# Loading x transposed by DMA instead of transposing it on TensorE, in a fused attention and MLP kernel

## The chip, the cores and the metric

The kernel runs on one core of a Trainium2 chip. The metric is the device time of one execution in microseconds (us). The core has five engines that work side by side, each through its own list of instructions in order: TensorE (PE, matmuls; its weight loads are shown apart as PEld), VectorE (DVE), ScalarE (ACT), GpSimd (POOL) and SyncE (SP). Here SP does nothing but issue DMAs; ACT issues a few as well. The engines meet through semaphores, that the layer in which the kernel is written places.

## The reference

With x of 2048 rows and 640 columns in bf16, 32 heads of 20, and F = 1536:

```python
def _A_ref(x, wqkv, wo):
    qkv = (x @ wqkv).reshape(B, S, 3, H, Dh)      # transposed to 3, B, H, S, Dh
    q, k, v = qkv[0], qkv[1], qkv[2]
    p = softmax(einsum("bhqd,bhkd->bhqk", q, k) * Dh ** -0.5)
    return einsum("bhqk,bhkd->bhqd", p, v) @ wo    # heads put back side by side
def _B_ref(x, w1, b1, w2):
    h = x @ w1 + b1
    return (h * tanh(softplus(h))) @ w2
x = A_x
g = sigmoid((x * gate_w).sum(-1, keepdims=True))
return g * _A_ref(x, A_wqkv, A_wo) + (1 - g) * _B_ref(x, B_w1, B_b1, B_w2)
```

## The kernel before

The 2048 queries are taken in four chunks of 512 and the 32 heads in eight sets of four (one head in each 32 rows of the PE array), which makes 32 groups G, one for each set and chunk. A group has 16 key tiles of 128 keys, and for each tile four scores, one a head: 64 score units of 128 x 512. A unit takes one of two ways. In batches of two or three it is exponentiated on ScalarE (L1051, into `E`), and P times V takes `E` (L1068). Or VectorE turns the scores into the bits of a power of two (L556, into `T`), GpSimd adds shifts to those bits as whole numbers (L586), and PV takes the shifted copies with values scaled accordingly (`VD`, L538). The 16-bit sums land in a PSUM bank `acc`; with each value tile goes a column of ones, whose sum is the softmax's denominator.

Everything runs in an order written out in the string `ORDER` (L19), read token by token at L1268 and issued just so (`manual_schedule`): nothing moves at run time, and an engine that waits holds up all that comes behind on it. The tokens used below:

- `S n,k`: a batch of n scores on PE into banks from k on; `x`: its exp on ScalarE.
- `D G,j,r,k`: one score on PE for the way over VectorE, `d G,k,two` opens such a key tile, `p` is an addition on GpSimd, `y` the next piece of VectorE's work.
- `V j,i`: PV of a key tile, four matmuls.
- `C n,bank` takes up chain n of a list sorted by due time, and each `F` runs its next piece on PE (four matmuls beside each other, L633, or five transposes, L643). Chains are the projections (K and Q strips, V in `v_chain`), the MLP's two products and the output product; the last piece hands a copy to VectorE. `v_chain` of the first four heads multiplies x by `wv0`, whose 81st column is `gate_w`, so that the gate's sum comes with it.
- `q`, `k`, `o`, `b`: loads on SP of Q, K (which went through DRAM to change their layout), of the attention's output (`od`, loaded transposed, L890) and of the MLP's result. `e0` computes the gate, `e1` loads wo. `H` are filler matmuls.

All products with x need x transposed (`xT`, 5 blocks kt of 128 columns, for all 2048 rows). The kernel loads x as it is into `xs`, views of the tile `big` that the MLP uses later. Chunk 0 comes in four loads, alternating between SP and ACT (L444), and is transposed at the start (L1156 to L1167) on PE, 20 transposes of 128 x 128 through PSUM, two copies on VectorE and two on ScalarE. Chunks 1 to 3 are loaded on SP (L451) and transposed by chains of one piece each (`transpose_chain`, L637), with a copy on VectorE (L651).

Ahead of `ORDER` stand the first projections for the heads 0 to 3 and chunk 0 (L1182): K with all 512 keys, then Q, 128 columns wide, since the unused rows of K's weight tile `wkp` carry other columns of K (`w_top`), which `store_top` writes to DRAM. Then the scores begin. The loads at the start go, in order of issue on SP: x of chunk 0, K's weights, `w_top`, x of chunk 1, the gate column (L457), x of chunk 2, a strip of Q's weights, x of chunk 3, a strip of K's, all of V's, the MLP's bias, w1, further strips, w1 again, w2.

After the last group PE adds the last two head sets' output product to what was computed before (L1284); the last 128 x 4 rows are copied from PSUM by ScalarE (two whole rows of blocks and a half) and VectorE (three halves) and stored by SP.

Of the kernel before, what the change touches and what calls it, by code (L numbers as in the profile page):

```python
# [9 lines left out]
P = 128  # L10
# [3 lines left out]
BF16 = mybir.dt.bfloat16  # L14
# [5 lines left out]
S2,0 S2,2 C1,6 F x C2,5 F y1 x C3,4 F y2 S2,0 y3 C4,6 F x S3,2 y4 C5,5 F F F F x F F F F F F F F F F F F S2,0  # L20
F F S3,2 x F F C0,6 F F y5 x y6 F y7 F y8 y9 F S2,0 y10 V0,-1 x V1,-1 V2,-1 C6,6 F F F F F V3,-1 C7,5 F y11
C8,4 F y12 S2,0 S2,2 q1 C9,6 F y13 x C10,5 F y14 C11,4 F F x F F y15 F S2,0 F F F F x F F F S2,2 F F F F x F
S2,0 S2,5 F F F x y16 C12,3 F y17 y18 F y19 F y20 F x S3,0 F V4,-1 x V5,-1 y21 V6,-1 C13,6 F S3,3 y22 C14,2 F
x S2,0 y23 C15,6 F C16,2 F x y24 S3,3 y25 V7,-1 C17,6 F x F F F F F F F F F S2,0 F F F F x F S3,2 F F F F F
C18,5 F x F y26 y27 F y28 S2,0 y29 y30 F F x S2,2 y31 V8,-1 V9,-1 x V10,-1 d1,0,1 S2,0 S2,4 d1,1,0 D1,15,0,6
d1,2,0 d1,3,0 x C19,3 F y32 F F F x S3,0 D1,15,3,6 F y33 V11,-1 x S2,4 y34 C20,6 F F F F F F F F F F F x F
S3,0 D1,14,0,3 F F F y35 F F x F F F S2,4 y36 C21,3 F y37 y38 F y39 y40 e0 F v0 y41 F x S3,0 D1,15,1,6 q2 y42
V12,-1 y43 F V13,-1 x V14,-1 y44 S2,4 D1,14,3,6 C22,3 F y45 F F x F S2,0 D1,15,2,2 V15,-1 y46 F x F F S2,4
D1,13,0,6 y47 F p1,4 F F x C23,2 F F y48 F S2,0 F y51 F x S2,4 D1,13,3,6 y52 F y49 F y50 F F F x V0,-1 S2,0
D1,14,1,3 V1,-1 y53 x p2,-1 V15,0 S2,4 y55 C24,6 F y56 x F y57 F S2,0 D1,14,2,2 y54 d1,4,0 F x S2,3 D1,12,0,5  # L30
y58 F V2,-1 y59 x V15,1 p3,5 S2,0 D1,13,1,2 y60 V3,-1 V14,0 x y61 p4,0 S2,3 D1,12,3,5 C25,6 V14,1 y62 F x S2,0
D1,13,2,2 d2,1,0 F y63 F x S3,3 F p5,5 F x V4,-1 S2,0 D1,12,2,2 y64 V14,2 V13,0 y65 V5,-1 p6,0 x V13,1 S3,3
D1,12,1,6 d2,5,0 V6,-1 y66 C26,2 F x F F V13,2 F S2,0 D1,11,0,6 p7,2 F F y67 F x F q3 S2,3 D1,11,1,5 p8,0
V12,0 y68 F F x S2,0 D1,11,3,6 V7,-1 y69 V12,1 y70 x V12,2 y71 S2,2 D1,11,2,5 D2,15,1,4 d2,0,0 V8,-1 y72 x
C27,6 F F S2,0 F y73 p9,2 F F x F S2,2 D2,15,2,5 F F y74 F p10,3 F x S2,0 D2,15,0,4 V11,0 y75 V9,-1 y76 x
V11,1 y77 S2,2 D2,14,1,6 D2,14,2,5 V11,2 y78 x V10,-1 S2,0 D2,15,3,4 d2,2,0 y80 C28,6 F x F S2,2 y79 V0,-1 x
y81 F S2,0 D2,14,0,5 F y82 p11,3 y83 F x S2,2 D2,13,1,4 V1,-1 y85 V15,0 p12,4 x S2,0 D2,14,3,5 y86 d2,6,0
V15,1 C29,6 F y87 x F S2,2 D2,13,2,4 V15,2 y84 F F x y88 p13,1 F S2,0 D2,13,0,5 F F y89 F x F S2,2 D2,12,1,4
p14,3 F V2,-1 y90 V14,0 x S2,0 D2,13,3,5 y91 d3,4,0 C30,4 F F y92 F x F y93 F S2,2 D2,12,2,6 F F y94 F x F
S2,0 D2,12,0,5 V3,-1 y95 F x V14,1 S2,2 D2,11,1,6 y96 p15,1 V14,2 y97 V4,-1 x y98 S2,0 D2,12,3,5 d3,3,0 V13,0  # L40
y99 V5,-1 x S3,2 D2,11,2,6 p16,-1 V13,1 y100 V6,-1 x V12,0 p17,1 S2,0 D2,11,0,5 V13,2 y101 C32,6 F F p18,0 x F
S3,2 D2,11,3,5 d3,5,0 F y102 x F V7,-1 V12,1 y103 S2,0 D3,15,1,5 p19,1 V12,2 y104 V8,-1 x S3,2 D3,15,0,6 V11,0
p20,0 y105 V11,1 x S2,0 D3,15,2,5 V9,-1 y106 C31,6 F F F x S3,2 D3,14,1,5 V11,2 y107 F x F S2,0 y108 V10,-1
C33,5 F F y109 x F S3,2 D3,14,2,6 F y110 y111 x F V0,-1 S2,0 y113 C34,6 F F F y112 F F x F S3,2 D3,15,3,5 q4
d3,0,0 F F y114 F x F V1,-1 V2,-1 y115 S2,0 D3,13,1,5 p21,1 y116 V15,0 y117 C35,6 F x F S3,2 k1 p22,2 F F F F
x F S2,0 D3,14,3,5 F F y118 F V15,1 V3,-1 x V15,2 y119 S3,2 D3,12,1,5 y120 V4,-1 v1 y121 C36,6 F x F F y122
S2,0 D3,14,0,5 y123 F y124 F x S3,2 V5,-1 y125 p23,1 V14,0 x C37,5 F S2,0 D3,13,0,6 F p24,2 y126 F F x d4,4,0
F S3,2 D3,13,3,6 y127 V14,1 x V6,-1 V14,2 y128 S2,0 D3,13,2,5 q5 d4,1,0 V7,-1 y129 C43,6 F x F S2,2 D3,12,0,4
p25,2 F y130 F x S2,0 D3,12,2,5 F p26,3 y131 V13,0 x S3,2 V8,-1 y132 V13,1 x S2,0 D3,12,3,5 d4,2,1 V13,2 y133
V9,-1 C38,6 F F x F p27,3 S3,2 D4,15,1,5 F y134 x F V10,-1 p28,5 V12,0 y135 S2,0 D4,15,0,5 V12,1 y136 x V12,2  # L50
S3,2 D4,15,2,6 V11,-1 y137 x C39,5 F F F y138 S2,0 D4,14,0,6 F y140 x F S3,2 V0,-1 y141 C40,6 F x F F y139 F
S2,0 D4,14,1,5 y142 F V1,-1 y143 x S3,2 y144 C41,5 F F x S2,0 D4,15,3,6 d4,0,0 F y145 F F V2,-1 x S2,2
D4,13,0,6 D4,13,1,4 y146 p29,3 V3,-1 V15,0 y147 x S2,0 D4,14,2,5 p30,5 V15,1 y148 C42,6 F x F y149 S2,2
D4,12,0,4 F y150 x F S2,0 D4,14,3,5 d5,3,0 V4,-1 q6 y151 F x S3,2 V15,2 y152 p31,4 V5,-1 x S2,0 D4,13,3,5
V14,0 y153 C44,6 F p32,5 F F x S3,2 D4,13,2,5 F y154 F x S2,0 V14,1 y155 p33,1 V6,-1 V14,2 C45,5 F F x F S3,2
D4,12,3,6 y156 F F x V7,-1 V8,-1 S2,0 y157 H p34,-1 V13,0 y158 x S3,2 D5,15,0,6 C46,5 F y159 F x F F S2,0
D4,12,2,6 F y160 V13,1 x V9,-1 S2,2 D4,12,1,4 y161 d5,1,0 V10,-1 C48,6 F x y162 S2,0 D5,15,2,5 F y163 p35,2 F
x S2,2 D5,15,1,4 V11,-1 y164 F x p36,4 S2,0 D5,15,3,5 d5,5,0 F y165 d5,6,1 V12,0 x V12,1 S3,2 y166 p37,0 V12,2
x C47,5 F S2,0 D5,14,0,6 y167 F p38,2 F y168 F x F y169 S3,2 y170 V0,-1 V15,0 x S2,0 D5,14,1,6 y171 V15,1 q7
q8 y172 V1,-1 V15,2 C49,5 F x S3,2 D5,14,3,6 F y173 F x F F S2,0 D5,14,2,6 y174 d6,0,0 V2,-1 V3,-1 x S3,2 y175  # L60
D5,13,0,5 C50,6 F p39,2 x y176 F F F F S2,0 D5,13,2,5 y177 p40,3 V4,-1 x V14,0 y178 S3,2 D5,13,1,6 V14,1 y179
V5,-1 x S2,0 D5,13,3,5 d6,1,0 V14,2 y180 C51,6 F F F x S3,2 D5,12,2,5 p41,2 F y181 F x V6,-1 V13,0 p42,3 y182
S2,0 D5,12,0,5 V13,1 y183 C52,6 F x S2,2 D5,12,3,4 F y184 F x F S2,0 D5,12,1,5 d6,2,0 F y185 x V7,-1 S3,2
V13,2 y186 p43,4 V8,-1 x S2,0 D6,15,1,5 V9,-1 y188 C53,6 F F F x y187 S3,2 D6,15,0,5 q9 F F x S2,0 y189 V10,-1
p44,-1 V12,0 y190 C54,5 F F x F S2,2 D6,14,0,4 V11,-1 y191 F x F S2,0 D6,15,2,6 y192 V12,1 C55,4 F y193 x S2,2
# [1275 lines left out]
```

## Time and profile before

| what | us |
|---|---|
| median of 3 runs (lowest to highest) | 697.27 (696.99 to 698.68) |
| the profiled execution | 697.02 |
| its span in the profile | 695.2 |
| first score on PE / first exp on ScalarE | 10.04 / 10.47 |
| end of the last exp | 686.7 |
| busy: PE / ACT / DVE / POOL | 680.5 / 676.6 / 582.0 / 339.6 |

The profile is of one execution; its span leaves out 1.8 us that lie around it in the measured time. Rows give the line of the kernel, the engine, the operation, what it writes and reads, and how often; a row of the timeline begins with the start in us and the time it covers, merged over so many instructions. The shapes are partitions x elements. PE's matmuls overlap: a row's mean duration is longer than the distance between two starts, and the latter is what counts for throughput; ScalarE's instructions overlap a little as well. In a table of stretches, each engine's busy time is followed by its number of instructions, and the last three columns are the granted clock of PE, the share of time in which the DMA engines were busy, and GB/s. What an engine waited for is inferred from semaphores.

### The profile page before, as it was taken

The numbers are of one execution on the slowest core, as the hardware profiler recorded it, in microseconds if no ns is written. First come the engines' busy times: TensorE is split into PE (matmuls) and PEld (weight loads), VectorE is DVE, ScalarE is ACT, GpSimd is POOL, SyncE is SP. The second block draws the span as 40 slices with busy tenths as digits, with TensorE's granted clock in tenths as the row PEclk, the third lists the DMA queues.
The fourth block names the chain that finished last, engine by engine and source line by source line (L and its number), as shares of the span: only waits on it lengthen the run. The fifth ranks groups of instructions, "written<-read, shape, count | busy, mean of one in ns | idle before, by whom it ended". The sixth has DMA issues, their size and how long they took to land.

```text
span 695.2 us, 24441 instructions
## 1 busy us (share of the span) xinstructions
PE 680.5 (98%) x10325; PEld 240.0 (35%) x10325; DVE 582.0 (84%) x1009; ACT 676.6 (97%) x665; POOL 339.6 (49%) x334
## 2 busy tenths in 40 slices
PE   8999999999999999999999999999999999999997
PEld 4433333332323343333333222222234333343333
DVE  4488868888799888788898999988989988888896
ACT  5899999999999999999999999999999999999996
POOL 5025443435365434544547555554643565545543
PEclk9999999999999999999999999999999999999999
DMA  9612132313211212112031214232222121143221
GB/s 249 194 15 46 32 75 52 58 51 85 50 26 33 67 37 40 27 38 56 24 83 36 43 32 90 44 67 57 37 63 81 22 50 29 41 74 61 58 58 48
DMA packets 125613, 40.46 MB, mean 58 GB/s; under 512 B 91136, under 2 KB 124944, under 8 KB 125504
## 3 DMA queue, kind: packets, MB, share of 16 engines
q1 hardware_dynamic: 123904, 38.38, 24.7%
q8 instruction: 80, 1.31, 0.8%
q10 hardware_dynamic: 1600, 0.53, 0.3%
q14 instruction: 29, 0.24, 0.1%
HBM read 23.61 MB, written 12.79 MB: 52 GB/s over the span
## 4 chain that ended last, share of the span: by engine, by line
PE 78%; ACT 15%; DVE 3%; issue 3%; DMA 1%; SPq 0%; DVEq 0%; ACTq 0%
PE Sp L1033 26%; PE Sp L1068 26%; PE Sp L633 24%; ACT E L1051 11%; ACT big L840 3%; DVE T L556 2%; DMA w_top<-in_A_wqkv_dram 1%; PE Sp L1284 0%; ACT L1051 0%; PE Sp L1184 0%; DVE VD L538 0%; DVE big L819 0%; DVE T L1111 0%; PE Sp L643 0%; DVE bt L864 0%
## 5 line engine op out<-in xcount | busy, mean ns | idle before, releaser
L1051 ACT ACTIVATE E<-Sp 128x1024 bf16<-128x1024 f32 (+1 forms) x650 | 645.5, 1175 | 5.1 <-PE Sp L1033 4.0
L586 POOL INT64_ADD T<-T x320 | 330.4, 1043 | 340.6 <-DVE T L556 195.8
L556 DVE TENSOR_SCALAR T<-Sp 128x512 int16<-128x512 f32 x640 | 425.0, 685 | 76.9 <-PE Sp L1033 67.3
L1033 PE MATMUL Sp<-qT,kT 32*128 32x512 bf16 x2048 | 260.4, 383 | 6.2 <-ACT E L1051 3.0
L1033 PEld LDWEIGHTS <-kT 32*128 32x128 bf16 x2048 | 71.5, 91 | 240.5 <-issue 236.0
L1068 PE MATMUL Sp<-E,VA 128*21 128x512 bf16 x1408 | 133.9, 383 | 0.0
L1068 PE MATMUL Sp<-T,VD 128*21 128x512 bf16 x1252 | 117.4, 382 | 0.2
L633 PE MATMUL Sp<-w_sb,big 128*32 128x320 bf16 x1536 | 74.2, 301 | 0.6 <-DVE T L556 0.5
L633 PE MATMUL Sp<-xT,w1t 128*32 128x512 bf16 x960 | 73.4, 383 | 0.2
L1068 PEld LDWEIGHTS <-VA 128*21 128x21 bf16 x2048 | 45.5, 90 | 63.3 <-issue 54.2
L1068 PE MATMUL Sp<-T,VA 128*21 128x512 bf16 x640 | 62.4, 381 | 0.0
L633 PE MATMUL Sp<-xT,ws 128*32 128x512 bf16 x720 | 52.3, 381 | 0.2 <-ACT E L1051 0.2
L633 PEld LDWEIGHTS <-big 128*32 128x32 bf16 x1536 | 35.0, 95 | 28.0 <-issue 19.6
L1068 PEld LDWEIGHTS <-VD 128*21 128x21 bf16 x1252 | 30.8, 90 | 39.1 <-issue 32.7
L819 DVE TENSOR_SCALAR big<-Sp,b1f 128x512 bf16<-128x512 f32 x48 | 35.6, 741 | 1.5 <-PE Sp L633 1.1
L633 PE MATMUL Sp<-wv,xT 128*32 128x81 bf16 (+2 forms) x960 | 33.3, 257 | 0.4 <-DVE st L721 0.2
L633 PE MATMUL Sp<-wo_sb,od 128*32 128x320 bf16 (+1 forms) x608 | 28.9, 301 | 0.6 <-DVE T L556 0.6
L633 PEld LDWEIGHTS <-w1t 128*32 128x32 bf16 x960 | 20.1, 95 | 26.3 <-issue 19.4
L721 DVE CAST st<-Sp 128x512 bf16<-128x512 f32 x36 | 24.7, 685 | 5.3 <-PE Sp L633 5.2
L633 PEld LDWEIGHTS <-xT 128*32 128x32 bf16 x960 | 19.1, 96 | 12.8 <-issue 9.2
L777 DVE CAST VA<-Sp 128x80 bf16<-128x80 f32 (+2 forms) x48 | 16.2, 373 | 8.2 <-PE Sp L633 8.2
L633 PEld LDWEIGHTS <-ws 128*32 128x32 bf16 x720 | 16.8, 95 | 17.7 <-issue 10.0
(75 smaller groups left out, 206.1 us busy)
## 6 DMA issues: line engine op xcount, KB each, us to landing
w1t<-in_B_w_dram SPq DMA_DIRECT2D x24, 320.0 KB
q_dram<-st SPq DMA_DIRECT2D x20, 128.0 KB
b_dram<-bt SPq DMA_DIRECT2D x16, 160.0 KB
bl<-b_dram SPq DMA_DIRECT2D x16, 160.0 KB
out_dram<-ot SPq DMA_DIRECT2D x16, 160.0 KB
qT<-q_dram SPq DMA_DIRECT2D x124, 20.0 KB
o_dram<-T SPq DMA_DIRECT2D x120, 20.0 KB
kT<-k_dram SPq DMA_DIRECT2D x28, 80.0 KB
```

Of the source, the lines that this page charges most:

```text
L556: nc.vector.tensor_scalar(out=dst.bitcast(I16), in0=src, scalar1=inv_sqrt_dh * LOG2E * 128.0, scalar2=127.0 * 128.0 + (BETA2 if two else B ...
L586: nc.gpsimd.int64_add(dst[:, :].bitcast(I64), src[:, :].bitcast(I64), n * 0x0001000100010001)
L633: nc.tensor.matmul(out_[k : k + 32], lhsT=lhsT[:, k : k + 32], rhs=rhs, tile_position=(0, k), **kw)
L721: nc.vector.tensor_copy(out=res["st"][:, :], in_=ps[:, :])
L777: nc.vector.tensor_copy(out=VA[:, sts[i], h0 : h0 + nh, 0:DH], in_=ps[:, i, 0:n].rearrange("p (h d) -> p h d", d=DH),)
L819: nc.vector.tensor_scalar(out=big[:, pair_of(c, ft), (ft % 2) * QC : (ft % 2 + 1) * QC], in0=ps[:, :], scalar1=b1f[:, ft : ft + 1], scalar ...
L840: nc.scalar.activation(v, v, ACT.Mish)
L1033: nc.tensor.matmul(ps_cols, lhsT=kT[p][32 * t_ : 32 * t_ + 32, j * P : (j + 1) * P], rhs=qT[G][32 * t_ : 32 * t_ + 32, :], tile_position=( ...
L1051: nc.scalar.activation(E[:, x : x + n, :], allb[:, k0 : k0 + n, :], ACT.Exp, scale=inv_sqrt_dh,)
L1068: nc.tensor.matmul(acc[32 * t_ : 32 * t_ + DH + 1, :], lhsT=lhsT, rhs=rhs, start=(pv_done[G] == 0), stop=(pv_done[G] == pv_total[G] - 1), ...
```

## The change

x is loaded transposed by DMA: for every chunk and block one `dma_start(transpose=True)` of 512 rows x 128 columns (`load_x`). For chunk 0 the five blocks alternate between SP and ACT, and the first weights for Q and K are issued on ACT ahead of them; chunks 1 to 3 are issued on SP, with a strip of weights behind each of the first two, the gate column behind that of chunk 1, and V's weights at the end. The transposes on PE, their copies and the chains that held them are gone.

The first projections become K for 256 keys alone (`AHEAD`, with the unused rows of `wkp` zero) and Q, block by block as x arrives; `w_top` is put into `wkp` after that, and a chain `first_k_chain(0, ...)` computes K of all of chunk 0 a second time, with `w_top`, whose store moves there too. One filler matmul (`NFILL`) goes.

The bias, w1, w2 and the second strips are loaded in `load_rest`, called with the gate (`e0`). At the end each of four blocks of 128 rows gets one copy of 640 columns, two on ScalarE and two on VectorE, and the third is stored from ACT's queue.

`ORDER` is written anew. It holds 842 `V` (825 before), 668 `D` (640), 647 exps (650), of which 561 are of two units and 86 of three (542 and 108), 1216 `F` (1223), 334 additions on GpSimd (320) and no `H` (3). `FIRST` and `EARLY` could reorder the first group's key tiles and split `make_vd`; with the values given they change nothing.

```diff
-    for u in range(NU):
-        eng = nc.sync if u % 2 == 0 else nc.scalar
-        eng.dma_start(out=xs[0][:, u, :], in_=x2d[u * P : (u + 1) * P, :])
-    load_first(1, nc.sync)
+    def load_x(c, kt, eng):
+        eng.dma_start(
+            out=xT[:, kt, c * QC : (c + 1) * QC],
+            in_=x2d[c * QC : (c + 1) * QC, kt * P : (kt + 1) * P],
+            transpose=True,
+        )
+
     load_first(0, nc.scalar)
-    nc.sync.dma_start(out=w_top[:, :, :], in_=wrows[:, :, D + KTOP : 2 * D])
+    load_first(1, nc.scalar)
+    for kt in range(KT):
+        load_x(0, kt, nc.scalar if kt % 2 else nc.sync)
+    nc.scalar.dma_start(out=w_top[:, :, :], in_=wrows[:, :, D + KTOP : 2 * D])
     nc.scalar.dma_start(out=wv0[:, :, 0 : 4 * DH], in_=wrows[:, :, 2 * D : 2 * D + 4 * DH])
...
+    for c in range(1, NQC):
+        for kt in range(KT):
+            load_x(c, kt, nc.sync)
+        if c < NQC - 1:
+            load_strip(c - 1, 0, nc.sync)
+        if c == 1:
+            nc.sync.dma_start(
+                out=wv0[:, :, 4 * DH : 4 * DH + 1],
+                in_=gate_w.rearrange("(kt p o) -> p kt o", p=P, o=1),
+            )
     nc.sync.dma_start(out=wv[:, :, :], in_=wrows[:, :, 2 * D : 3 * D])
-    nc.sync.dma_start(b1bf, B_b1.rearrange("(ft p) -> p ft", p=P))
-    load_w1(0)
-    load_strip(0, 1, nc.sync)
-    load_strip(1, 1, nc.sync)
-    load_w1(1)
-    nc.sync.dma_start(out=w2_sb[:, :, :], in_=B_w2.rearrange("(ft p) c -> p ft c", p=P))
+
+    def load_rest():
+        load_strip(0, 1, nc.sync)
+        load_strip(1, 1, nc.sync)
+        nc.sync.dma_start(b1bf, B_b1.rearrange("(ft p) -> p ft", p=P))
+        load_w1(0)
+        load_w1(1)
+        nc.sync.dma_start(out=w2_sb[:, :, :], in_=B_w2.rearrange("(ft p) c -> p ft c", p=P))
...
-    sb = [bank_ap(g, [P, QC]) for g in (6, 2)]
+    pad_copy(wqp, w_first[0][:, :, :])
+    pad_copy(wkp, w_first[1][:, :, :])
...
-    for w, dst, k in ((wkp, kT[0][:, 0:QC], 0), (wqp, qT[0][:, :], 1)):
-        for kt in range(KT):
+    firsts = [
+        (bank_ap(4, [P, AHEAD]), wkp, kT[0][:, 0:AHEAD], nc.vector.tensor_copy),
+        (bank_ap(1, [P, QC]), wqp, qT[0][:, :], nc.scalar.copy),
+    ]
+    for kt in range(KT):
+        for ps, w, dst, _ in firsts:
             nc.tensor.matmul(
...
+    for ps, _, dst, copy in firsts:
+        copy(out=dst, in_=ps)
+    nc.vector.tensor_copy(
+        out=wkp[:, :, :, DH:32], in_=w_top[:, :, :].rearrange("p k (h d) -> p k h d", h=4)
+    )
...
     def gate_values():
+        load_rest()
...
+    finish(0, nc.scalar.copy, nc.sync)
+    finish(1, nc.vector.tensor_copy, nc.sync)
+    finish(2, nc.scalar.copy, nc.scalar)
+    finish(3, nc.vector.tensor_copy, nc.sync)
```

The new `ORDER` begins so, with the chains that stand behind the numbers C1 (K of chunk 0 again), C2 (`v_chain` of chunk 0, with the gate column), C0 (Q of chunk 1) and C3 (K of chunk 1):

```
S2,0 S2,2 C1,6 F x F F F F x C2,5 F F F F y1 F F F F F F F F S2,0 S2,2 F x F F F F F F F y3 S2,0 x y4 y5 y6 y7
y2 V0,-1 x S3,2 V1,-1 C0,6 F x F F F S2,0 F x C3,5 F F y8 F F F V2,-1 C4,6 F y9 F F F F F F F F F F F S3,0
```

More of the change, by code (lines that the diff above doesn't have):

```diff
@@ L25 @@
[L25 to L29, printed above, removed]
@@ L334 @@
     NSB = 2
-    NFILL = 1
+    FIRST = (0, 1, 2, 3, 4, 5, 6, 7, 8, 9, 10, 11, 12, 13, 14, 15)
+    EARLY = 16
+    AHEAD = 2 * P
     NSH = len(SHIFT) - 1
@@ L532, with tile_of, make_vd @@
     VD = {}
-    def make_vd(p):
-        VD[p] = work.tile([P, ND, NSH, 4 * (DH + 1)], BF16, tag=f"VD{p % NLAST}", name="VD")
+    def tile_of(p, j):
+        return FIRST[j] if p == 0 else j
+    def make_vd(p, part):
+        if p not in VD:
+            VD[p] = work.tile([P, ND, NSH, 4 * (DH + 1)], BF16, tag=f"VD{p % NLAST}", name="VD")
+        lo, hi = NS - ND, NS
+        if p == 0:
+            lo, hi = ((lo, EARLY), (EARLY, hi))[part]
+        j0 = tile_of(p, lo)
         def scale(i):
             nc.vector.tensor_scalar(
-                out=VD[p][:, :, i, :],
-                in0=VA[:, NS - ND : NS, 4 * p : 4 * p + 4, :].rearrange("p j h d -> p j (h d)"),
+                out=VD[p][:, lo - (NS - ND) : hi - (NS - ND), i, :],
+                in0=VA[:, j0 : j0 + hi - lo, 4 * p : 4 * p + 4, :].rearrange("p j h d -> p j (h d)"),
                 scalar1=RATIO[i + 1], scalar2=None, op0=ALU.mult,
@@ L953, in spread @@
         return [(a + (b - a) * k / n, a + (b - a) * (k + 1) / n) for k in range(n)]
+    chains.append(first_k_chain(0, -1.0, -0.3))
     for c in range(1, NQC):
-        for u in range(NU):
-            chains.append(transpose_chain(NU * c + u, -1.0, 0.25 * c - 0.2 + 0.01 * u))
         chains.append(first_k_chain(c, -1.0, 0.25 * c - 0.1))
@@ L1032, in score @@
         p = groups[G][0]
+        j = tile_of(p, j)
         nc.tensor.matmul(
@@ L1153 @@
     o_last = {}
[L1156 to L1179 removed]
+    pad_copy(wqp, w_first[0][:, :, :])
+    pad_copy(wkp, w_first[1][:, :, :])
     kT[0] = kTb[0]
     qT[0] = qTb[0]
[L1182 to L1183 removed]
+    firsts = [
[4 more added lines that the diff above has]
+        for ps, w, dst, _ in firsts:
             nc.tensor.matmul(
[L1185 removed]
+                ps,
                 lhsT=w[:, kt, :, :].rearrange("p h d -> p (h d)"),
[L1187 removed]
+                rhs=xT[:, kt, 0 : ps.shape[1]],
                 start=(kt == 0),
```

622 lines of the change are left out of this document (280 added, 342 removed).

## The prediction

> **What bounds the kernel now.** I read the page first, then the chain of waits, the groups by shape, the timelines of the start and of the end, and the transposing loads. The page's busy shares and its chain (the whole lines, three engines first):
>
> ```profile
> PE 680.5 (98%) x10325; PEld 240.0 (35%) x10325; DVE 582.0 (84%) x1009; ACT 676.6 (97%) x665; POOL 339.6 (49%) x334
> ...
> PE 78%; ACT 15%; DVE 3%; issue 3%; DMA 1%; SPq 0%; DVEq 0%; ACTq 0%
> ```
>
> TensorE (PE) is the bound, with ScalarE (ACT) close behind. A busy PE says little by itself, so I took the distances from one matmul's start to the next, slot by slot along ORDER. When nothing waits: one `V` (4 matmuls) 0.216 us, a piece `F` of 512 columns 0.216, of 320 0.136, of 240 0.103, of 81 0.039; a score batch `S` alone 0.32, but 0.007 when a `D` follows it (they run in the same pass), and that `D` 0.314; after an `F` or `V`, going to `S` costs 0.105 more. Added along the old list this gives 654.2 us; its first score starts at 10.04 and its last slot is 677.0 later. So 22.8 us are waits of PE, 9.9 of them in front of `S` or what then takes its bank.
>
> ScalarE, by shape; beside it the DVE work that takes its place:
>
> ```profile
> L1051 ACT ACTIVATE E<-Sp 128x1024 bf16<-128x1024 f32 x542 | 521.6, 1102 | 4.6 <-PE Sp L1033 3.7 <-ACT E L1051 0.2
> L556 DVE TENSOR_SCALAR T<-Sp 128x512 int16<-128x512 f32 x640 | 425.0, 685 | 76.9 <-PE Sp L1033 67.3 <-POOL T L586 1.3 <-issue 0.2
> ...
> L1051 ACT ACTIVATE E<-Sp 128x1536 bf16<-128x1536 f32 x108 | 166.6, 1543 | 0.5 <-PE Sp L1033 0.4
> ```
>
> Instructions overlap at their ends: back to back, an exp of 1024 starts 0.904 us after the one before, one of 1536 makes it 1.331. So the exps need 542 x 0.904 + 108 x 1.331 = 633.7 us.
>
> The start, from the timeline:
>
> ```profile
> 1.21 2.74 PE L493 MATMUL Sp<-qT 128*128 128x512 bf16 x6 [1.21 <-DVE qT L478]
> ...
> 4.26 0.51 SPq L457 DMA_DIRECT2D wv<-in_gate_w_dram  x1
> ...
> 7.03 1.25 PE L1184 MATMUL Sp<-xT,wkp 128*128 128x512 bf16 x5 [0.53 <-DVE wkp L1171]
> ...
> 8.12 1.24 PE L1184 MATMUL Sp<-xT,wqp 128*128 128x512 bf16 x5
> ...
> 10.04 0.40 PE L1033 MATMUL Sp<-qT,kT 32*128 32x512 bf16 x4 [0.67 <-ACT qT L1192]
> ...
> 10.47 7.38 ACT L1051 ACTIVATE E<-Sp 128x1024 bf16<-128x1024 f32 x7 [0.48 <-PE Sp L1033]
> ```
>
> The first exp is at 10.47, after x, its 20 transposes, K and Q. L493 spends 0.43 us per matmul, L1184 0.216 on the same width: PE starts at half pace, though the granted clock reads 1.00. The gate column is asked for at 4.26 and has landed by 9.6, before its first reader.
>
> Transposing loads, which the kernel has already for `od` (same block, 512 x 128 from rows of 1280 bytes). First answer: the timeline of SyncE (SP), two places; second: a table of stretches around the lone one:
>
> ```profile
> 489.05 5.12 SPq L890 DMA_TRANSPOSE od<-o_dram  x4
> ```
>
> ```profile
> 578.50 1.56 SPq L890 DMA_TRANSPOSE od<-o_dram  x1
> ```
>
> ```profile
> 579.50:580.00 0.50, 0.50 (x11) 0.22 (x11) 0.00 (x0) 0.50 (x1) 0.50 (x1) 1.00 0.35 82
> 580.00:580.50 0.50, 0.50 (x16) 0.21 (x8) 0.50 (x1) 0.50 (x2) 0.38 (x1) 1.00 0.79 173
> 580.50:581.00 0.50, 0.50 (x14) 0.23 (x14) 0.20 (x1) 0.50 (x1) 0.13 (x1) 1.00 0.06 7
> ```
>
> Issuing one holds its queue 1.2 to 1.3 us (a plain load: 0.4 to 0.5). The lone one moves its bytes between 579.5 and 580.7, and its completion counts are in by 581.2: 2.7 us from the start of its issue.
>
> **The change, part by part.**
>
> *The list.* The same distances along the new ORDER give 650.7, 3.5 less: the 12 transposes of later chunks go (-4.1); `V` 825 to 842, with their turns to `S` (+5.4); `D` 640 to 668 (+3.7); score batches, fewer of them alone (-6.3); five pieces more for K of chunk 0, the rest of that chunk's keys (+0.9); three `H` (-0.7); pieces of other widths, fewer turns (-2.3). ScalarE: 561 x 0.904 + 86 x 1.331 = 621.6, 12.1 less, since 28 more score units go over DVE. DVE gets 28 x 0.664 = 18.6 us more and loses 14 copies of 0.49; it idles 113 us, which covers it; were it not covered, it would cost these 12 us. POOL gets 14 adds of 1.04 and is half idle.
>
> What of ScalarE's 12.1 shows is bounded by nothing (PE leads the chain with 78%) and by all 9.9 of the waits in front of `S`. PE's work falls by 0.5%, ScalarE's by 1.9%, so I take half: -4.9.
>
> *x by DMA, chunk 0.* Five transposes, kt 0, 2, 4 on SP and 1, 3 on ACT. The trace of before has all its transposes on one queue, so it can't show what two queues do. Bounds: side by side, SP issues three in 3 x 1.25 us, so the last starts at 3.25 and lands at 5.95; one at a time, each issued when the one before it has landed, 0.73 + 5 x 2.7 = 14.2. I take the second: the code alternates the queues at every block, and I expect the layer that places this program's semaphores to put one in front of each change of queue; the trace of before doesn't decide it, hence the large chance of B below. [...]
>
> [...]
>
> From the last landing to the first score: before, the last Q matmul starts at 8.99 and the score at 10.04, 1.05; PE has been idle between blocks and may be at L493's pace, and a quarter of K comes too: 1.4. First score 15.6, against 10.04 (+5.6).
>
> *The gate column.* It moves behind the five transposes of chunk 1 and a weight strip on SP. SP starts kt 4 at 11.5; six transposes x 1.27 = 7.6; the strip 0.5: the gate load starts at 19.6 and lands, by the same 2.7, at 22.3. The new list puts v_chain of chunk 0 (C2), whose right-hand side holds that column, 1.4 us of work after the first score, at 17.0. PE runs in order, and behind C2's first piece stand the scores for the third and fourth exp. So all engines stop for 5.3 us; nothing covers it. [...]
>
> Chunk 1 has landed by 21 and its strip before the gate column; chunks 2 and 3 land near 29 and 35, wanted 9.8 and 15.5 us of work after 22.3. Covered by 3 us.
>
> *w1, w2, late strips with the gate (`e0`).* They leave the start of SP and come 28 us of work after the first score, in front of Q loads; a strip is wanted 24 us later, w1 55. 0; if the cover goes, the 6 us that 1.9 MB take at the 329 GB/s that the stretch from 20 to 25 us shows.
>
> *The end.*
>
> ```profile
> 690.12 1.29 ACT L1299 CAST ot<-Sp 128x640 bf16<-128x640 f32 x2 [3.42 <-PE Sp L1284]
> ...
> 690.68 1.29 DVE L1308 CAST ot<-Sp 128x320 bf16<-128x320 f32 x3 [0.47 <-PE Sp L1284]
> 690.84 0.93 SPq L1302 DMA_DIRECT2D out_dram<-ot  x2
> 691.29 0.44 ACT L1306 CAST ot<-Sp 128x320 bf16<-128x320 f32 x1
> 691.86 0.89 SPq L1310 DMA_DIRECT2D out_dram<-ot  x2
> ```
>
> SP issues the last store at 692.36. Two copies of 640 columns on each engine end near 691.9 (DVE: 0.82 each, from 0.69 for 512), and one store goes by ACT's queue: the last issue near 691.95, -0.4.
>
> **Sum**, against the profiled execution's 697.02 us (span 695.2 and 1.8 around it; the median of the runs is 697.27): 15.6 + 650.7 + 22.8 waits + 5.3 + 1.0 - 4.9 = 690.5 for the end of the list, before 687.0: +3.5; the end -0.4: +3.1. **700 us**.
>
> **The rivals.**
>
> *B, the transposes run side by side (other side).* First score 5.95 + 1.4 = 7.4; gate column issued at 4.5 + 6.35 + 0.5 = 11.35, landing 14.05, still a stop of 5.25. 7.4 + 673.5 + 5.25 + 1.0 - 4.9 = 682.3, -4.7, with the end -5.1: 692. For it: nothing in the trace of before shows such a wait. It decides when the second queue's transpose starts under 1.4 us after the first's. Without relief of ScalarE 697.
>
> *C, ScalarE paces the whole.* Most of its exps start exactly 0.904 apart, which speaks for it. Then all 12.1 us come back in place of 3.5 + 4.9: 3.7 better than the forecast, 696.3. Against: 78% PE.
>
> *D, SP jams.* After 20.1: ten transposes, 12.7, strip, wv, four o_dram stores (3.2), then 8 stores of K rows and the store and load of group 1's Q: landing between 47 and 53. Group 1's first score is 28.4 - 1.4 us of work after 22.3, 50.3 with the slow clock. At worst 3 to 4 us late, with both engines empty: 704. Before, these had no 20 slow issues ahead of them.
>
> **How the numbers follow.** Forecast 0.50, B 0.24, C 0.14, D 0.12. The forecast's own range is 697 to 704 (relief 0 to 9.9, slow clock 0 to 2). Range over all: 691 to 705.5. About 0.3%, 2.1 us, is what can be told from no change here. Slower by more: 0.37 of the forecast's 0.50, D's 0.12, 0.01 of C: 0.50. Faster: 0.20 of B, 0.04 of C, 0.02 of the forecast: 0.26. Within: 0.24.
>
> **What would show it.** Right: five transposes of x alternating on SP and ACT about 2.7 us apart, first exp near 16, an idle PE of some 5 us in front of the first xT x wv piece with the gate's load as its releaser, exps near 622 us at their own pace, a PE list near 651 plus waits. Wrong: transposes 1.25 us apart and the first exp near 8 (B); no stop at the gate column; or PE waits well off 18 to 23 us in the rest.

## The result, and the profile after

The changed kernel takes 707.27 us (median of 4 runs, 705.93 to 707.97), the kernel before 697.94 in the same session: 1.0135 times as long, with a 95% interval of 1.0123 to 1.0147. The prediction was 700.0 with a range of 691 to 705.5. The time lies above that range. So the sign was right and the size was not: +3.1 us was forecast, and in the profiled execution it is +10.4 (span 705.6 against 695.2).

The page, engines and the chain that ended last:

```profile
PE 676.8 (96%) x10320; PEld 236.1 (33%) x10320; DVE 588.7 (83%) x1021; ACT 665.1 (94%) x659; POOL 357.0 (51%) x349
...
PE 74%; ACT 14%; issue 3%; DVE 3%; DMA 3%; SPq 1%; DVEq 0%; ACTq 0%
```

Every engine that bounds the kernel is busy for less time than before (PE 680.5, ACT 676.6), and the span is longer: the time went into pauses. DMA and SP now hold 4% of the chain, 1% before. The exps, by shape:

```profile
L1043 ACT ACTIVATE E<-Sp 128x1024 bf16<-128x1024 f32 x561 | 535.3, 1088 | 15.5 <-PE Sp L1025 14.3
...
L1043 ACT ACTIVATE E<-Sp 128x1536 bf16<-128x1536 f32 x86 | 131.0, 1525 | 1.6 <-PE Sp L1025 1.6
```

In the kernel before, ScalarE idled 4.6 us ahead of its exps of 1024 (3.7 of them for PE); now it is 15.5 (14.3 for PE). Where, the chain of waits over the first 30 us shows (start, length, what held it):

```profile
0.73 1.23 SPq L445
...
3.30 3.09 DMA xT<-in_A_x_dram
...
6.50 2.67 DMA xT<-in_A_x_dram
...
9.19 2.52 DMA xT<-in_A_x_dram
...
11.73 2.67 DMA xT<-in_A_x_dram
...
14.47 1.12 SPq L445
...
20.18 3.03 DMA wv<-in_gate_w_dram
```

SP issues three blocks of x at its own pace (0.73, 2.01, 3.30). Then each change of queue waits until the transposes before it have landed: ACT at 6.50, SP at 9.19 (this is already a block of chunk 1), ACT at 11.73, SP at 14.47. The same start as a timeline, on PE and ScalarE:

```profile
16.55 0.61 PE L1025 MATMUL Sp<-qT,kT 32*128 32x512 bf16 x4 [0.67 <-ACT qT L1166]
17.09 2.32 PE L647 MATMUL Sp<-xT,wkp 128*32 128x512 bf16 x20
17.19 1.94 ACT L1043 ACTIVATE E<-Sp 128x1024 bf16<-128x1024 f32 x2 [0.70 <-PE Sp L1025]
...
23.25 1.01 PE L647 MATMUL Sp<-wv,xT 128*32 128x81 bf16 x48 [3.83 <-DMA wv<-in_gate_w_dram]
...
24.84 4.26 ACT L1043 ACTIVATE E<-Sp 128x1024 bf16<-128x1024 f32 x4 [5.71 <-PE Sp L1025]
```

First exp at 17.19 (10.47 before); the stop at the gate column is there, PE idle 3.8 us and ScalarE 5.7. The five `F` of C1 at 17.09 cover 2.32 us; at full pace they take 1.3 (0.216 each and the last one's length): PE is at half pace.

Laid out as the prediction's sum was, with distances between starts on PE and their minimum when nothing waits:

| part of the span, us | before | after | difference | predicted |
|---|---|---|---|---|
| first score starts | 10.04 | 16.55 | +6.5 | +5.6 |
| the list at its minimum | 654.2 | 650.65 | -3.5 | -3.5 |
| PE's waits up to 40 us | 2.9 | 7.9 | +5.0 | +6.3 |
| waits from 40 to 60 us | 0.9 | 4.2 | +3.3 | 0 |
| waits after 60 us | 19.0 | 17.1 | -1.9 | -4.9 |
| last slot to the end | 8.25 | 9.2 | +1.0 | -0.4 |
| sum | | | +10.4 | +3.1 |

The stop behind "from 40 to 60 us" is one the prediction didn't see. The timeline there:

```profile
54.16 0.26 ACT L1184 ACTIVATE g_t<-z_t 128x16 f32<-128x16 f32 x1
...
54.45 0.17 DVE L1185 TENSOR_SCALAR g_t<-g_t 128x16 f32<-128x16 f32 x1 [0.92 <-ACT g_t L1184]
...
55.03 0.69 DVE L713 CAST st<-Sp 128x512 bf16<-128x512 f32 x1
...
55.77 0.29 PE L647 MATMUL Sp<-wv,xT 128*32 128x240 bf16 x4 [1.81 <-DVE st L713]
```

The gate's steps stand in DVE's queue ahead of the copy that frees PE's bank, and their first one waits for the gate's exp, which stands in ScalarE's queue behind the exps of scores. And the stop is paid a second time, as a table of stretches shows (busy time and number of instructions of PE, PEld, DVE, ACT and POOL, then granted clock, DMA share, GB/s):

```profile
56.00:58.00 2.00, 2.00 (x38) 0.91 (x38) 1.19 (x3) 1.18 (x2) 0.00 (x0) 0.67 1.06 144
58.00:60.00 2.00, 2.00 (x27) 0.39 (x17) 1.79 (x4) 1.62 (x2) 1.39 (x2) 0.50 0.85 243
60.00:62.00 2.00, 2.00 (x54) 1.15 (x50) 1.81 (x4) 1.67 (x3) 0.67 (x1) 0.98 0.97 251
```

From 56.7 to 60.1 PE has half its clock, which makes 1.4 us more: of the 3.3 that this stretch lost, 1.9 are the stop and 1.4 the clock. e4 below has the same stop without the slow clock (its mean granted clock is 0.999) and loses 1.7 there against the kernel before.

The end, timeline:

```profile
698.00 1.11 PE L1259 MATMUL Sp<-wo,O 128*128 128x320 bf16 x7 [1.05 <-DVE big L928]
...
700.03 1.25 PE L1259 MATMUL Sp<-wo,O 128*128 128x320 bf16 x8
700.56 0.69 ACT L1276 CAST ot<-Sp 128x640 bf16<-128x640 f32 x1 [5.29 <-PE Sp L1259]
700.87 1.56 DVE L1276 CAST ot<-Sp 128x640 bf16<-128x640 f32 x2 [1.53 <-PE Sp L1259]
701.28 1.51 SPq L1279 DMA_DIRECT2D out_dram<-ot  x3
701.79 0.69 ACT L1276 CAST ot<-Sp 128x640 bf16<-128x640 f32 x1 [0.54 <-DVE ot L1276]
```

PE's final products wait 1.05 us for copies of the last output chains (C177 to C179), which the new list runs up to its last tokens. From the start of the last eight matmuls to the end of the span it is 5.56 us (5.66 before). ScalarE's second copy waits 0.54 for DVE's; no run shows why.

### The profile page after: what moved, and what is told of

The parts are those of the page before. It is cut to its first block, busy times and chain, and to the rows that moved or that the text cites. A ratio compares the mean times of both kernels' runs of the same rounds, so it can differ in the third digit from the quotient of the medians.

```text
span 705.6 us, 24501 instructions
## 1 busy us (share of the span) xinstructions
PE 676.8 (96%) x10320; PEld 236.1 (33%) x10320; DVE 588.7 (83%) x1021; ACT 665.1 (94%) x659; POOL 357.0 (51%) x349
## 4 chain that ended last, share of the span: by engine, by line
PE 74%; ACT 14%; issue 3%; DVE 3%; DMA 3%; SPq 1%; DVEq 0%; ACTq 0%
PE Sp L1060 25%; PE Sp L1025 25%; PE Sp L647 23%; ACT E L1043 13%; DVE T L570 2%; DMA xT<-in_A_x_dram 2%; ACT big L832 1%; SPq L445 1%; DMA q_dram<-st 1%; DMA wv<-in_gate_w_dram 0%; PE Sp L1259 0%; DVE st L713 0%; DVE big L811 0%; DVE T L1089 0%; DVE big L928 0%
## 5 line engine op out<-in xcount | busy, mean ns | idle before, releaser
L1043 ACT ACTIVATE E<-Sp 128x1024 bf16<-128x1024 f32 (+1 forms) x647 | 635.6, 1146 | 17.0 <-PE Sp L1025 15.9
L600 POOL INT64_ADD T<-T x334 | 347.2, 1051 | 324.8 <-DVE T L570 184.3
L570 DVE TENSOR_SCALAR T<-Sp 128x512 int16<-128x512 f32 x668 | 440.6, 684 | 63.2 <-PE Sp L1025 53.3
L1025 PE MATMUL Sp<-qT,kT 32*128 32x512 bf16 x2048 | 257.0, 386 | 5.9 <-DVE st L713 1.9
L1025 PEld LDWEIGHTS <-kT 32*128 32x128 bf16 x2048 | 68.9, 91 | 238.9 <-issue 235.9
L1060 PE MATMUL Sp<-T,VD 128*21 128x512 bf16 x1320 | 125.1, 382 | 0.0
L647 PE MATMUL Sp<-xT,w1t 128*32 128x512 bf16 x960 | 75.2, 383 | 0.1
L647 PE MATMUL Sp<-w_sb,big 128*32 128x320 bf16 x1536 | 72.5, 301 | 0.3 <-DVE ot L928 0.2
L1060 PE MATMUL Sp<-T,VA 128*21 128x512 bf16 x668 | 64.9, 382 | 0.0
L1060 PEld LDWEIGHTS <-VD 128*21 128x21 bf16 x1320 | 32.3, 90 | 39.1 <-issue 32.8
L647 PEld LDWEIGHTS <-ws 128*32 128x32 bf16 x720 | 17.0, 96 | 18.9 <-issue 10.2
```

Of the source, the lines that this page charges most:

```text
L570: nc.vector.tensor_scalar(out=dst.bitcast(I16), in0=src, scalar1=inv_sqrt_dh * LOG2E * 128.0, scalar2=127.0 * 128.0 + (BETA2 if two else B ...
L600: nc.gpsimd.int64_add(dst[:, :].bitcast(I64), src[:, :].bitcast(I64), n * 0x0001000100010001)
L647: nc.tensor.matmul(out_[k : k + 32], lhsT=lhsT[:, k : k + 32], rhs=rhs, tile_position=(0, k), **kw)
L1025: nc.tensor.matmul(ps_cols, lhsT=kT[p][32 * t_ : 32 * t_ + 32, j * P : (j + 1) * P], rhs=qT[G][32 * t_ : 32 * t_ + 32, :], tile_position=( ...
L1043: nc.scalar.activation(E[:, x : x + n, :], allb[:, k0 : k0 + n, :], ACT.Exp, scale=inv_sqrt_dh,)
L1060: nc.tensor.matmul(acc[32 * t_ : 32 * t_ + DH + 1, :], lhsT=lhsT, rhs=rhs, start=(pv_done[G] == 0), stop=(pv_done[G] == pv_total[G] - 1), ...
```

## Experiments

The ratios are against the kernel before, run beside each (medians 696.95 to 697.02). All but e11 start from the changed kernel, which was timed in a session where the kernel before took 1 us more; so differences from it are taken from ratios, or from e7, which lies within 0.04% of it by its ratio and ran beside e5, e6 and e8.

| kernel | us (lowest to highest) | ratio, 95% | first score | waits to 40 / 40 to 60 |
|---|---|---|---|---|
| e1_one_queue | 701.98 (701.06 to 703.18) | 1.0073 (1.0058 to 1.0088) | 10.12 | 9.6 / 3.2 |
| e2_gate_early | 700.95 (699.53 to 702.97) | 1.0059 (1.0036 to 1.0083) | 12.27 | 6.4 / 2.5 |
| e3_both | 701.27 (698.00 to 702.14) | 1.0069 (1.0052 to 1.0086) | 10.08 | 6.6 / 3.1 |
| e4_x_plain | 694.14 (692.18 to 695.64) | 0.9956 (0.9941 to 0.9972) | 10.50 | 3.2 / 2.6 |
| e5_filler | 706.38 (704.68 to 706.77) | 1.0129 (1.0112 to 1.0146) | 15.67 | 5.5 / 3.8 |
| e6_gate_steps_later | 704.71 (703.73 to 705.62) | 1.0109 (1.0094 to 1.0125) | 16.08 | 7.8 / 1.4 |
| e7_old_end | 706.62 (706.39 to 707.26) | 1.0139 (1.0123 to 1.0154) | 16.10 | 8.0 / 3.9 |
| e8_chunk0_on_PE | 695.25 (692.99 to 698.29) | 0.9973 (0.9955 to 0.9990) | 9.10 | 7.2 / 3.9 |
| e9_filler_more | 706.86 (704.05 to 707.33) | 1.0130 (1.0104 to 1.0156) | 15.71 | 2.1 / 5.5 |
| e10_best | 692.08 (691.56 to 692.93) | 0.9930 (0.9913 to 0.9948) | 8.92 | 4.5 / 0.8 |
| e11_exp_shorter | 690.36 (690.26 to 692.55) | 0.9913 (0.9896 to 0.9930) | 9.92 | 4.8 / 0.7 |
| e12_all_dma_mended | 695.37 (694.21 to 696.20) | 0.9974 (0.9963 to 0.9985) | 10.05 | 6.9 / 1.2 |

The last two columns are of the one profiled execution of each, and a wait counts where it begins (the stop of e8 at 40 us in the first of the two numbers). This execution isn't always a typical one: it is the fastest of e1, e2 and e3, and the slowest of e6, e8, e11 and e12.

**The queues and the gate column.** e1: `load_x(0, kt, nc.sync)` for all five blocks. e2: the gate column's `dma_start` moved ahead of the loop over chunks 1 to 3. e3: both.

> All five transposing loads of chunk 0 go on SP, nothing else changes. If the hand-over between the queues is what delays the start (each change of queue waits about 2.7 us for a landing), the five are issued 1.28 us apart, the last lands near 8.6, the first score comes near 10.0 instead of 16.55, and the gate column near 16.8 instead of 23.2, with the same stop of 4 to 5 us in front of it: about 700.8 us, 6.5 less than the changed kernel, still above the kernel before. If the DMA engines or HBM set the pace of the transposes, whatever the queue, the last block still lands near 14.4 and the time stays at 707.

> The gate column is loaded on SP ahead of the transposes of chunk 1, the blocks of chunk 0 still alternate. If the stop of PE from 18.8 to 23.2 is owed to the gate column, it goes, and the scores of the third exp follow the second at once: 4 us earlier there, and some of the half-paced matmuls after the pause with it. If nothing behind it is late, about 703; if the loads and stores queued on SP are late anyway (the staging tiles are freed by stores that stand behind the transposes), a later wait takes the gain back and the time stays near 707.

> One queue for chunk 0 and the gate column early. First score near 10, no stop at the gate: PE is some 10.5 us ahead of the changed kernel at its 20th exp. SP gains only the 6 us of the hand-overs, so the wait for a staging tile near the 40th exp (2.2 us in the changed kernel) should grow to some 5 or 6: about 700, little better than with one queue alone. If SP's queue is not what that wait is owed to, the gains add up: about 696.

e1 takes 4.3 us off (0.62 points of the ratio) and the first score comes 6.4 us earlier. But the gate column still stands behind chunk 1's five transposes and a strip, so the stop there grows from 4.3 to 5.8 us above its minimum:

```profile
17.34 1.01 PE L647 MATMUL Sp<-wv,xT 128*32 128x81 bf16 x48 [5.63 <-DMA wv<-in_gate_w_dram]
```

e2 does two things at once. The stop at the gate is gone, and ACT's two blocks go out together behind SP's three (issues at 6.10 and 7.33), since SP's next transpose now follows them: first score 12.27. e3 doesn't add the two gains. What follows is next in line: PE now stops 3.1 us at 14.8 for the first strip of Q's weights, which SP issues behind chunk 1's transposes, and 1.6 at 44.0 for group 1's Q, which stands further back on SP.

**No transposing at all.** e4: one plain load a chunk, gate early.

```diff
+            out=xT[:, :, c * QC : (c + 1) * QC],
+            in_=x2d[c * QC : (c + 1) * QC, :].rearrange("(p a) d -> p (a d)", p=P).rearrange("p (k q) -> p k q", q=QC),
```

> x is loaded by one plain load a chunk, into the shape of xT but not transposed, so all products with x have other values (the computation is the same in size); the gate column comes early. This takes the transposes' price away and leaves the new list and the new end. If the loads at the start are the whole loss: first score near 7, no wait for the gate, no wait for staging tiles, 650.7 us of list with some 19 of waits and 9 of end: about 688 us, 10 below the kernel before. If the new list itself is worse (its VectorE share, its waits), 695 or more.

694.14: with x free of any transposing, the change is 2.8 us better than the kernel before, far from the 688 that would make the loads at the start the whole loss, and its first score, 10.50, is no earlier. The ten K and Q matmuls run at half pace there (0.64 for a pair of 768 columns), behind a pause of PE from 4 to 6.4 us for the padded weights, where the kernel before transposes x on it. The pause alone doesn't settle the pace: in e12 it is 2.2 us long, and a pair after it takes 0.32 (6.68 to 7.00). The rest of what the change could win is eaten by the gate's steps (1.9 above the minimum at 42.3) and the late end.

**The slow pace.** e5: 26 fillers `matmul(acc, warm_z, warm_z)` in three pauses; e9: 4 more at the start, and 51.

> The changed kernel with 26 filler matmuls (128 x 512, written to the bank of acc, which is idle then) in the three early pauses of PE: 5 ahead of the second block of x, 9 ahead of the fourth, 12 ahead of the first piece that reads the gate column. Theory 'the pauses also slow the clock': the changed kernel's PE needs 0.43 us for a 512-column matmul from 6 to 29 us, twice the 0.216 of the same matmuls later; of its waits before 40 us some 3.7 us are this half pace. With PE kept busy the pace is 0.216 again, the first score comes 0.4 us earlier, and the whole takes about 704.5 us, 2.8 less than the 707.3 of the changed kernel. Rival 'the half pace only fills waits that are there anyway' (for the gate column, for ScalarE): within 0.5 of 707.3. Fillers that overrun their pause would make it slower by up to 1 us.

> The changed kernel with more fillers than e5_filler, which left PE empty for 3.2 us ahead of the gate column and at half pace after it: 10 matmuls at the very start in place of 6, 9 ahead of the second block of x, 18 ahead of the fourth, 24 ahead of the first piece that reads the gate column. Theory 'a pause of 3 us or more halves PE's pace for the next 5 to 9 us': without a pause the matmuls after the gate column take 0.216 and not 0.43 per 512 columns, and the 1.8 us that e5_filler still lost between 20 and 30 us go to under 0.5: about 704.8 us, some 1.5 less than e5_filler's 706.4 and 2.5 less than the changed kernel's 707.3. Rival 'the pace doesn't hang on the pause' or 'what half pace costs there is waiting anyway': 706.4, or more if the fillers overrun.

e5 is 0.2 us under e7, as its rival had it, but its fillers ended 2.8 us before the gate column came, and from 25.3 to 28.8 PE was at half pace again. e9 does what its theory wanted: full pace after the gate column, waits before 40 us 2.1 in place of 7.9 (some of it turned into the fillers' own 5.2). The same `V` slot starts at 49.18, where e7 has 50.28. So the half pace costs about 1.1 us up to there. Yet the whole takes 706.86, as much as e7:

```profile
49.87 2.83 SPq L741 DMA_DIRECT2D qT<-q_dram  x4
50.58 0.39 PE L1025 MATMUL Sp<-qT,kT 32*128 32x512 bf16 x3
...
53.33 0.38 PE L1025 MATMUL Sp<-qT,kT 32*128 32x512 bf16 x1 [2.36 <-DMA qT<-q_dram]
```

SP is no earlier: its queue (chunk 3's transposes, V's weights, 4 stores of zeros, 16 of K's rows) reaches the load of group 1's Q at 49.87, and the gain is given back there. Theory and rival both miss: with PE kept busy the pace stayed full (the granted clock reads 1.00 from 4.6 to 55.8), and this does not show in the time as long as SP is late.

**The gate's steps.** e6 makes what follows the gate's exp a step of its own, which a new token calls one exp later in `ORDER`:

```diff
         nc.scalar.activation(g_t[:, :], z_t[:, :], ACT.Exp, scale=-1.0)
+
+    def gate_rest():
         nc.vector.tensor_scalar(out=g_t, in0=g_t, scalar1=1.0, scalar2=None, op0=ALU.add)
```

> The changed kernel with the gate split: its loads and the exp on ScalarE stay at e0, the three steps on DVE and the gate's stores and loads come one exp later in ORDER, when ScalarE's exp is done. Theory 'DVE queue': PE's stop of 2.2 us at 53.6 (1.87 above its minimum) comes from DVE, which waits at the gate's first step for ScalarE's exp, with the copy behind it that frees PE's bank; then the stop goes and the whole takes about 705.4 us. Rival 'the copy is late for another reason, ScalarE's or SP's lateness': 707.3, with the stop still there.

704.71, 1.9 less than e7 in the same session, as the theory had it. (Its profiled execution, 705.62, gains 2.5 us between 40 and 60 us and loses part of it later: from 254.2 its clock is halved for 3.4 us, with a mean clock of 0.998 where the three other runs have 1.000, which e7's is not.) The stop is gone: the copy is at its place and PE's piece waits 0.22 for it, while the gate's first step comes 1.5 us after its exp began:

```profile
53.05 0.68 DVE L713 CAST st<-Sp 128x512 bf16<-128x512 f32 x1
...
53.66 0.26 ACT L1184 ACTIVATE g_t<-z_t 128x16 f32<-128x16 f32 x1
...
53.78 0.29 PE L647 MATMUL Sp<-wv,xT 128*32 128x240 bf16 x4 [0.22 <-DVE st L713]
...
55.17 0.17 DVE L1187 TENSOR_SCALAR g_t<-g_t 128x16 f32<-128x16 f32 x1
```

**The end.** e7 puts the old copies and stores back.

> The changed kernel with the old end (two copies of 640 on ScalarE, three of 320 on DVE, one of 320 on ScalarE, all stores from SP). The prediction gave the four-copy end -0.4 us: then this takes 707.7 us. Theory 'the end itself is worth nothing': from the first final matmul to the end took 5.57 us after and 5.62 before, so 707.3 (within 0.1 of it in the profile's last stretch, 5.6 us from the first final matmul). Either way the last stretch of the list to the end stays about 9.2 us, since the lateness (1.0 us against before) comes from the output product's chains ahead of it.

The ratio is that of the changed kernel; in the profile the last eight matmuls to the end take 5.61 us (5.56 with four copies). The four-copy end is worth nothing that shows, and the 1.0 us of a late end stays with either. That it is due to the place of the last output chains in the list is read from the trace; no run moved them.

**The relief of ScalarE.** e11, on the kernel before: `E[:, x : x + n, 0:496]` from `allb[:, k0 : k0 + n, 0:496]`.

> The kernel before with ScalarE's exps over 496 of each 512 columns (the last 16 queries of each chunk are left out of what ScalarE adds): PE and DVE do the same work, ScalarE 19.4 us less by the profile's rows (0.861 ns a column, 1408 units). It tests the prediction's term 'relief of ScalarE', which took half of the 9.9 us of PE's waits in front of scores as coming back when ScalarE has 12.1 us less. By that term at least 4.9 us come back: 692 or less. Rival 'these waits are for the order of the banks and for DVE, not for ScalarE's pace', as the changed kernel showed (1.9 us less waits from 60 us on): 695 to 696.

```profile
L1052 ACT ACTIVATE E<-Sp 128x992 bf16<-128x992 f32 x542 | 503.7, 1010 | 8.3 <-PE Sp L1034 5.8 <-ACT E L1052 0.4 <-PE Sp L1069 0.2
...
L1052 ACT ACTIVATE E<-Sp 128x1488 bf16<-128x1488 f32 x108 | 154.0, 1426 | 3.2 <-PE Sp L1034 2.6
```

Back to back, the exps start 0.878 us apart in place of 0.904 (1.291 for 1.331), some 18 us in all, and the kernel is 6.6 us faster. After 60 us PE's waits in front of scores fall from 9.1 to 2.7 us, those in front of `D` and `F` don't move. So the mechanism that the prediction named exists, and the rival falls. Its price is about 0.36 us (6.6 / 18.4) for each us that ScalarE gets lighter than PE.

**Mended versions.** e8: chunk 0 loaded plain and transposed on PE as before, gate column early, chunks 1 to 3 by transposing loads on SP, gate's steps late. e10: e8, and

```diff
+    load_strip(0, 0, nc.sync)
     for c in range(1, NQC):
...
+    def late_stores():
...
+        for c in range(NQC):
+            store_top(c)
```

`late_stores` holds the stores of zeros to `o_dram` and of K's rows, and is called behind the loads of group 6's Q.

e12: e10 with all of x by transposing loads, on SP alone.

> The changed kernel with chunk 0 of x loaded as it is and transposed on PE at the start, as in the kernel before (20 transposes, two copies each on DVE and ScalarE); the gate column issued on SP ahead of chunk 1; chunks 1 to 3 by transposing loads on SP alone; the gate's steps on DVE one exp later. Theory 'the new list is good, its start is what costs': first score 10.0, list 650.7, waits 2.9 before 40 us as in the kernel before, 0.7 from 40 to 60, 16.7 after that, 9.2 from the list's last slot to the end: 689.5 span, 691.3 us, faster than the kernel before (697). Rival 'SP is too late for the new list in any case' (chunk 1 by DMA lands after its first reader at 14.8 or so): 3 us more waits, 694.

> e8_chunk0_on_PE with two changes on SP's queue: the first strip of Q's weights is loaded ahead of chunk 1's transposing loads, and the 20 stores that nothing reads for a long time (rows of K, zeros of the output) move from in front of group 1's Q to behind group 6's. In e8_chunk0_on_PE PE stood 3.7 us for group 1's Q (at 39.9) with its granted clock at 0.50 for 9 us after it (another 3.7), and 2.4 us were lost between 10 and 20 us, mostly for the strip. Theory 'SP's queue is what is late, and each long stop is paid twice': those stops go, 10 to 60 us then has about 3 us of waits in all, first score 9.1, list 650.7, after 60 us 16.5, end 9.1: 688.4 span, about 690 us, in every run (e8_chunk0_on_PE spread from 693.0 to 698.3). Rival 'something else waits there' (copies on DVE, ScalarE): 693.

> e3_both (all of x by transposing loads on SP alone, the gate column ahead of chunk 1) with what mended e8_chunk0_on_PE: the first strip of Q's weights ahead of chunk 1's transposes, the 20 late stores moved behind group 6's Q, the gate's steps on DVE one exp later. It differs from e10_best only in how chunk 0 of x comes. Theory 'with SP's queue in order the change costs only what its first score and its late chunk 1 cost': first score 10.1 (e10_best 8.9), chunk 1 some 3.5 us later on SP than in e10_best and wanted about 1 us later, so 2 to 3 us more waits: span 692 to 693, 694 us, faster than the kernel before by 0.4%. Rival 'chunks 2 and 3 come late as well, and each stop is paid twice by the clock': 697 or more, no faster than before.

e8 starts earlier than the kernel before (9.10) and then stops for group 1's Q; the timeline, and the table of stretches:

```profile
39.83 1.74 SPq L680 DMA_DIRECT2D k_dram<-kT  x4
...
41.67 1.39 SPq L741 DMA_DIRECT2D qT<-q_dram  x4
...
43.58 0.60 PE L1025 MATMUL Sp<-qT,kT 32*128 32x512 bf16 x1 [3.29 <-DMA qT<-q_dram]
```

```profile
40.00:45.00 5.00, 1.71 (x16) 0.39 (x13) 0.69 (x1) 1.97 (x3) 0.00 (x0) 0.70 0.28 86
45.00:50.00 5.00, 5.00 (x60) 1.61 (x52) 3.65 (x9) 2.96 (x3) 0.48 (x1) 0.50 0.67 139
50.00:55.00 5.00, 5.00 (x79) 1.99 (x80) 4.27 (x10) 3.86 (x4) 1.57 (x2) 0.77 0.78 214
55.00:60.00 5.00, 4.97 (x72) 1.44 (x60) 4.79 (x10) 4.99 (x7) 4.12 (x4) 1.00 0.97 330
```

The stop costs 3.7 us and the clock at 0.50 behind it another 3.8: in this execution it is paid twice. The ten executions go from 692.99, at a mean granted clock of 0.999, to the 698.29 shown here, at 0.990, so the slow clock does not come with every one. The median, 695.25, is above both the theory's 691.3 and the rival's 694. With 20 stores out of the way (e10) the load is issued at 33.86, both losses go, and 692.08 us is faster than either kernel, 0.70% under the one before. It is 2 us above the theory's 690 and nearer the rival's 693. But what waits now is no copy: PE waits for the last block of chunk 3, which is as fast as SP can issue 15 transposes:

```profile
20.28 7.07 SPq L445 DMA_TRANSPOSE xT<-in_A_x_dram  x5
27.39 1.33 SPq L468 DMA_DIRECT2D wv<-in_A_wqkv_dram  x1
...
29.36 0.93 PE L648 MATMUL Sp<-xT,wkp 128*32 128x512 bf16 x8 [1.63 <-DMA xT<-in_A_x_dram]
```

e12, between its theory's 694 and its rival's 697, is 3.3 us slower than e10: five transposes more on SP push chunk 3 to 31.3, the first score comes 1.1 later, and PE's clock is halved from 7.9 to 14.7. In its best arrangement tried here the change as it was meant is 0.26% faster than the kernel before, and with chunk 0 left on PE 0.70%. How much of this the transposing loads bring is not shown: no run gives the late stores to the kernel before.

## Why the prediction went wrong

Two steps failed: the relief of ScalarE, put at -4.9 and measured as -1.9, and the work that moves to `e0`, put at 0 and measured as +3.3 between 40 and 60 us. The other terms are off by less.

**The start** was right in kind. It named a wait at each change of queue, 2.7 us each, against rival B; the runs show 2.5 to 3.1, and e1 removes them. That the last block lands at 14.4 against 14.2 is luck in part. The sum took five landings one after another; here SP issues three blocks without waiting (two steps of 1.28), then four landings follow, and one of them is a block of chunk 1 in between. In e2, where ACT's two blocks go together, SP goes on at 10.2, when the last of the five has landed. In both traces no transpose of one queue starts while one of the other is under way: in the changed kernel the issues at 6.50, 9.19, 11.73 and 14.47 follow landings at 6.39, 9.17, 11.71 and 14.39, in e2 those at 6.10 and 10.21 follow landings at 6.00 and 10.12. From the last landing of the five to the first score the changed kernel took 2.2 us in place of 1.4. In e5, at full pace, it took 1.7: so about 0.4 of it is the half pace, and the rest that two blocks (kt 3 and 4) are multiplied behind the last landing. Together they are most of the 0.9 us that the term lacked.

**The gate column**: the stop was forecast as 5.3 us and is 4.3; the load was issued at 20.2 (19.6 forecast), but PE came to it 1.8 us later than forecast.

**The slow clock** behind the gate column: the sum has 1.0 us for it, from a range of 0 to 2. This term was the author's estimate, and no run shows it for that stop alone; e9 shows 1.1 for the whole start. The 3.7 us that the later expectation read from the spacing were too much: most of the half pace lay where PE would have waited for ScalarE or a DMA anyway. What the prediction lacked is that the clock fell again behind a later stop (0.50 from 56.7 to 60.1 in the changed kernel, 1.4 us).

**The relief, -4.9**, is the largest term that was mis-sized: -1.9 came. The step "I take half" of the waits in front of scores had no row behind it. e11 gives the price: 0.36 us for each us. The new list takes 12.1 us from ScalarE, but 3.5 from PE too, so ScalarE gained 8.6 on PE, worth 3.1 by that price (an estimate: the price is from 18.4 us, not from 8.6); the waits in front of scores fell by 1.8 (9.1 to 7.3). Why not all of the 3.1 came is open.

**"w1, w2, late strips with the gate: 0"** is the step that failed outright. The loads themselves cost nothing that a run shows, but the prediction looked only at what `e0` puts on SP and not at what its compute steps meet in the queues of ScalarE and DVE at their new place in `ORDER`: a stop of 1.9 us and a slow clock behind it, 1.9 in time (e6 against e7).

**The end, -0.4**: the copies bring 0.05 to 0.1, since ScalarE's second one waits for DVE, and the last slots to the end take 1.0 us more, by the trace for the place of the last output chains, which the prediction had not looked at.

**Rival D, SP's jam**, was right about the resource and hidden by the rest: in the changed kernel PE comes late enough not to wait for it. As soon as PE is made faster (e3, e8, e9), it waits there, 1.6 to 3.7 us. **Rival C** doesn't hold: ScalarE idles 11 us more in front of its exps of 1024.

So the forecast of +3.1 lacked 3.0 in the relief, 3.3 in the stop of the gate's steps and what goes with it, 1.4 at the end and 0.9 at the start, and had 1.3 too much at the gate column and the slow clock behind it.

## What to carry to other kernels

Where an order is written by hand, go through every engine's queue at the place to which a step is moved, not the step's DMAs alone: a short chain across two engines (ScalarE's exp, DVE's sums) that is put ahead of a copy on which PE waits costs the lag between these engines (1.9 us here, e6 against e7). Take transposing off PE only when the DMA queue has room for it: here the 20 blocks of a chunk took PE 1.6 us back to back (e8) at the start, when it had nothing else to do, and the five transposing loads in their place take 1.26 us of SP each. Removing a wait is worth what is late next, so look at that queue before the wait is priced: e1, e2 and e3 each won 4 to 5 us, not the sum.

## What the runs showed of the hardware

- In the changed kernel a transposing load of 512 x 128 held the queue that issued it for 1.26 us (the median of 18 on SP, 1.12 to 2.09), and those ahead of a change of queue landed 2.52 to 3.09 us after their issue began. Each of the four changes waited for such a landing; with all five blocks on one queue (e1) the first score came 6.4 us earlier.
- Behind some pauses of PE its granted clock fell to 0.50, for 3.4 us or for two, three or five times as long. It was 3.4 us in the changed kernel (56.7 to 60.1, behind a pause of 1.8), e5, e9 and e10 (pauses of 2.8, 2.4 and 1.6), 6.8 in e12, 10.2 in e1 and e8 (pauses of 5.6 and 3.3) and 17.1 in e2. In the changed kernel it set in 0.9 us after PE had gone on (55.77 to 56.7), in e9 2.5 (53.33 to 55.8). The pause alone doesn't decide: one of 1.8 us left the clock alone in e4, and in e8 it also fell at 14.7, behind no single pause above 0.4. With fillers in the early pauses it stayed at 1.00 up to 55.8 (e9). Matmuls of 512 columns start 0.427 us apart at half pace and 0.216 at full pace.
- In both traces the granted clock has no record at the start, and the tables print 1.00 there. In the changed kernel the first record is at 29.4 us: from 17 to 29 us the table reads 1.00 while the matmuls start 0.427 us apart. In the kernel before it is at 6.9, which is why the prediction met half pace at a clock of 1.00. There the distance between starts is the sign to go by.
- DVE's copy of Q's weights (128x400) takes 2.17 us in the changed kernel beside GpSimd's memset of `VA`, and 0.26 to 0.27 in e8 and the kernel before, where it comes after that memset. e1, e2 and e4 have the slow one too; no run separates it from what else differs.
